# Batch 0: other queues and places for v's second half, the first w_in loads, the decay transposes and the first GEMM blocks

## The chip, the cores and the metric

The kernel runs on one core of a Trainium2 chip. The core has a matrix engine (TensorE, PE in the profile; its weight loads are PEld), VectorE (DVE), ScalarE (ACT), GpSimd (POOL) and SyncE (SP), each with its own instruction queue that is worked off in order, and 16 DMA engines that all queues of transfers share. SyncE and GpSimd both issue transfers here. The metric is the device time of one execution in microseconds: before the change the median of three runs is 336.82 us (336.6 to 336.88).

## The reference, cut to what matters

Attention with a forget gate on 8 batches, 8 heads, 576 tokens and 64 columns a head, and then an MLP with exact GELU on the 4608 tokens of 512 columns:

```python
scores = scale * np.matmul(q, k.transpose(0, 1, 3, 2))
log_f = np.log(np.clip(f, 0.0001, 1.0))
cum = np.cumsum(log_f, axis=-1)
decay = cum[:, :, :, None] - cum[:, :, None, :]
scores = np.where(causal, -1000000000.0, scores + decay)
attn = softmax(scores)
x = np.matmul(attn, v)                      # heads side by side: 4608 x 512
h = x @ w_in                                # 512 -> 2048
out = (0.5 * h * (1.0 + erf(h / sqrt(2)))) @ w_out   # 2048 -> 512
```

## The kernel before, in words

The order of all work is written out by hand; each engine runs its instructions in program order, and waits are put where data or buffers need them.

**Tiling.** A batch's 576 tokens are five blocks of up to 128 keys (`K0` = 0, 128, 256, 384, 448; the last one overlaps and only its upper 64 rows count). Heads go in four pairs `i` of 128 columns. Scores stand with keys on the partitions: TensorE writes `s`, ScalarE's exponential gives `e` in bf16. The decay is taken into v: `wT` holds a weight for each key and head, and `weigh_v` multiplies v by it into `vw`, whose 65th column is the weight itself, so that the product of `e` and `vw` (`o`) gives numerator and denominator at once. VectorE divides, giving `x`; TensorE transposes `x` into a PSUM tile `ps_x`, which is copied into `xT`. `gemm1` multiplies `xT` by a 128-column block `ffb` of w_in, four contraction steps `kt` of one pair each, and ScalarE's GELU makes `g`; the second GEMM multiplies `g` by w_out.

**Stages.** Batch 0 (`first_attention`) is attention alone, since nothing else is there yet to compute. Each later batch's attention is interleaved with the second GEMM of the batch before. The change is all in batch 0 and in the loads that precede it.

**Loads.** GpSimd issues q and k (converted to bf16 on the way) in four pieces each for batch 0, then all of w_in and w_out. `load_v` (line 114) makes one transfer for each block of keys, 128 KB for four heads. Lines 157 to 159 give SyncE nine of them: blocks 0 to 3 of heads 0 to 3, the same of heads 4 to 7, and block 4 of all heads. They come after GpSimd's memset of one column of `v_sb` (line 156).

**Batch 0 in order.** TensorE transposes q and k by pairs (`transposes(i, 0)` for q, `transposes(i, 1)` for k), computes scores in pieces (`scores_a`, `scores_b`, `scores_c`, `scores_t`, `scores_t4`), and transposes `decay` into `psw` by five small transposes (lines 711 to 715), from which VectorE copies `wT`. `keep()` is a filler: one matmul of 512 columns into a tile that nobody reads (ps_w, line 720). VectorE weighs v for heads 0 to 3 (lines 740, 741), GpSimd for heads 4 to 7 (lines 746, 747), and block 4 of all heads in one product (line 749). GpSimd's first two w_in loads stand behind the "gate" of lines 742 and 743, a copy of one column that must wait for block 3 of v's first four heads. Behind them in GpSimd's queue come the two weighings, w_in(2), the product of block 4, batch 1's first q and k, a memset of v's column for batch 1 and batch 1's v. `attend_0(i, h)` is the product of `e` and `vw` for one head; `to_xT_0(i, copy)` transposes and copies x of pair i.

**PSUM.** Three pools of two buffers each: `s_psum` (two banks a buffer) for scores, `o_psum` for attention products ("AV"; `spare()` takes one for a GEMM block), and `m_psum` for transposes and GEMM blocks.

**Into the first GEMM.** Lines 781 to 787: blocks 0, 1 and 2 are begun with their first three contraction steps, block 0 in `m_psum`, 1 and 2 in the halves of one `s_psum` tile `more`; then x of pair 3 is transposed and copied; then the three blocks get their fourth step, each followed by its GELU; block 3 is done whole. After block 4 comes `attend_tail` (the last 64 queries) and after block 5 `tail_0`.

Of the kernel before, what the change touches and what calls it, by code (L numbers as in the profile page):

```python
# [9 lines left out]
FP32 = mybir.dt.float32  # L10
# [5 lines left out]
P = 128  # L16
# [3 lines left out]
HP = 4  # L20
NBLK = 5
# [32 lines left out]
def kernel(  # L54
# [10 lines left out]
    nc = tc.nc  # L65
# [20 lines left out]
    x_pool = ctx.enter_context(tc.tile_pool(name="x", bufs=3))  # L86
# [27 lines left out]
    v_sb = consts.tile([P, H, NBLK, D], FP32)  # L114

    def load_v(b, h0=0, h1=H, eng=nc.sync, ns=range(NBLK)):
        if b >= B:
            return
        for n in ns:
            p0 = D if n == NBLK - 1 else 0  # L120
            eng.dma_start(
                v_sb[p0:P, h0:h1, n, :],
                v[b, h0:h1, K0[n] + p0 : K0[n] + P].rearrange("h p d -> p h d"),
            )
# [30 lines left out]
    diagonal(ident_fp, Alu.not_equal, 1.0, 0)  # L155
    nc.gpsimd.memset(v_sb[:, :, 0, 0:1], 0.0)
    load_v(0, 0, 4, ns=range(4))
    load_v(0, 4, 8, ns=range(4))
    load_v(0, ns=[NBLK - 1])

    qT = [consts.tile([P, S], BF16, name=f"qT{i}") for i in range(HP)]
    kT = [consts.tile([P, S], BF16, name=f"kT{i}") for i in range(HP)]
# [6 lines left out]
    def load_w_in(c):  # L169
        f4 = slice(c * d_ff // 4, (c + 1) * d_ff // 4)  # L170
        nc.gpsimd.dma_start(w_in_sb[:, :, f4], w_in_r[:, :, f4])
# [20 lines left out]
    def warm_up(n, w=TC):  # L192

        ps = m_psum.tile([P, TC], FP32, tag="m", name="ps_w")
        for _ in range(n):
            nc.tensor.matmul(
                ps[:, 0:w], warm[:, 0:P], warm[:, 0:w], start=True, stop=True
            )
# [4 lines left out]
    def transposes_first(b, i, which, pool, tag, parts=1):  # L203

        src = qk_of[b][which]
        ps = pool.tile([P, JT, PT], BF16, tag=tag, name="ps_f")
        for j in range(JT):
            for h in range(2):
                nc.tensor.transpose(  # L209
                    ps[h * D : (h + 1) * D, j, :],  # L210
                    src[:, 2 * i + h, j * D : (j + 1) * D],
                    ident_bf[:PT, :PT],
                )

        dst = (qT, kT)[which][i].rearrange("d (p j) -> d p j", j=JT)
        src = ps.rearrange("d j p -> d p j")
        if b or i:
            for p in range(parts):
                part = slice(p * PT // parts, (p + 1) * PT // parts)
                nc.vector.tensor_copy(dst[:, part], src[:, part])  # L220
        else:
            nc.vector.tensor_copy(dst[:, 0 : PT // 2], src[:, 0 : PT // 2])
            nc.scalar.copy(dst[:, PT // 2 :], src[:, PT // 2 :])
# [36 lines left out]
    def vw(b):  # L260
        if b not in vw_of:
            vw_of[b] = v_pool.tile([P, H, NBLK, D + 1], BF16, tag="vw", name=f"vw{b}")
        return vw_of[b]

    def weigh_v(b, i, eng=nc.gpsimd, n0=0, n1=NBLK):

        hs = slice(2 * i, 2 * i + 2)
        bh = b * H + 2 * i
        w = wT[:, n0:n1, bh : bh + 2].rearrange("p n h -> p h n")
        eng.tensor_tensor(  # L270
            vw(b)[:, hs, n0:n1, 0:D],
            v_sb[:, hs, n0:n1, :],
            w.unsqueeze(3).to_broadcast([P, 2, n1 - n0, D]),
            Alu.mult,
        )
        if b:
            eng.tensor_copy(vw(b)[:, hs, :, D], w)
# [75 lines left out]
    def xT(b):  # L353
        if b not in xT_of:
            xT_of[b] = xT_pool.tile([P, n_dm, XC], BF16, tag="xT", name="xT")
        return xT_of[b]
# [25 lines left out]
    def gemm1(c, ffb, kts=range(4), ps=None, act=True):  # L382
        src = xT(c) if c < B else tails
        if ps is None:
            ps = m_psum.tile([P, TC], FP32, tag="m", name="ps1")
        for kt in kts:
            nc.tensor.matmul(  # L387
                ps,
                w_in_sb[:, kt, ffb * P : (ffb + 1) * P],
                src[:, kt, 0:TC],  # L390
                start=(kt == 0),
                stop=(kt == n_dm - 1),
            )
        if n_dm - 1 in kts and act:
            gelu(c, ffb, ps)
        return ps

    def spare():
        return o_psum.tile([P, TC], FP32, tag="o", name="ps1")

    def gelu(c, ffb, ps):
        if c not in g_of:
            g_of[c] = [
                g_pool.tile([P, TC], BF16, tag=f"g{n}", name=f"g{n}")
                for n in range(n_ff)
            ]
        nc.scalar.activation(g_of[c][ffb], ps, Act.Gelu)  # L407
# [203 lines left out]
    def scores_a(i):  # L611
        scores_0([(i, 0, 0, TC)], new_e(0))

    def scores_b(i):
        scores_0([(i, 1, P, TC - P), (i, 3, 3 * P, P)], new_e(2))

    def scores_c(i):
        scores_0([(i, 2, 2 * P, 2 * P), (i + 1, 2, 2 * P, 2 * P)], new_e(3))

    def scores_t(i):  # L620
        parts = [(ii, n, TC, TL) for ii in (i, i + 1) for n in range(NBLK - 1)]
        scores_0(parts, new_e(3))

    def scores_t4():
        scores_0([(i, NBLK - 1, TC, TL) for i in range(HP)], e4[0][:, :, D:])
# [62 lines left out]
    def first_attention():  # L688

        most = NBLK - 1  # L690

        def transposes(i, which, parts=1):
            transposes_first(0, i, which, m_psum, "m", parts)

        warm_up(9)
        for which in range(2):
            transposes_first(0, 0, which, o_psum, "o")
        nc.vector.tensor_tensor_scan(
            decay[:, S - 2 :: -1],
            f_sb[:, S - 1 : 0 : -1],  # L700
            none[:, 0 : S - 1],
            2.0**80,
            Alu.mult,
            Alu.add,
        )
        warm_up(2, 2 * P)
        scores_a(0)
        scores_b(0)
        transposes(1, 0)
        transposes(1, 1, 2)  # L710
        psw = o_psum.tile([P, NBLK, BH], FP32, tag="o", name="psw")
        for n in range(NBLK):
            nc.tensor.transpose(
                psw[:, n, :], decay[:, K0[n] : K0[n] + P], ident_fp[:BH, :BH]
            )
        idle = o_psum.tile([P, TC], FP32, tag="o", name="ps_w")

        def keep(n=1):
            for _ in range(n):
                nc.tensor.matmul(idle, warm[:, 0:P], warm, start=True, stop=True)  # L720

        keep()
        scores_a(1)
        nc.vector.tensor_copy(wT[:, 0:4, :], psw[:, 0:4, :])
        nc.vector.tensor_copy(wT[D:P, 4, :], psw[D:P, 4, :])
        nc.vector.tensor_copy(
            vw(0)[:, :, :, D], wT[:, :, 0:H].rearrange("p n h -> p h n")
        )
        transposes(2, 0)
        scores_b(1)  # L730
        transposes(2, 1)
        keep()
        scores_c(0)
        transposes(3, 0)
        keep()
        scores_a(2)
        transposes(3, 1)
        keep()
        scores_b(2)
        weigh_v(0, 0, nc.vector, 0, most)  # L740
        weigh_v(0, 1, nc.vector, 0, most)
        g = x_pool.tile([P, 1], FP32, tag="gate", name="gate")
        nc.gpsimd.tensor_copy(g, v_sb[:, 3, most - 1, 0:1])
        load_w_in(0)
        load_w_in(1)
        weigh_v(0, 2, n1=most)
        weigh_v(0, 3, n1=most)
        load_w_in(2)
        nc.gpsimd.tensor_tensor(
            vw(0)[:, :, most, 0:D],  # L750
            v_sb[:, :, most, :],
            wT[:, most, 0:H].unsqueeze(2).to_broadcast([P, H, D]),
            Alu.mult,
        )
        load_qk_tokens(1, 0, 4)
        nc.gpsimd.memset(v_sb[:, :, 0, 0:1], 0.0)
        load_v(1, 0, 4, nc.gpsimd)
        load_w_in(3)
        load_qk_tokens(1, 4, 8)
        load_v(1, 4, 8, nc.gpsimd)  # L760
        keep()
        scores_a(3)
        keep()
        attend_0(0, 0)
        attend_0(0, 1)
        scores_b(3)
        scores_c(2)
        attend_0(1, 0)
        attend_0(1, 1)
        to_xT_0(0, nc.scalar.copy)  # L770
        scores_t(0)
        attend_0(2, 0)
        attend_0(2, 1)
        to_xT_0(1, nc.scalar.copy)
        scores_t(2)
        attend_0(3, 0)
        to_xT_0(2, nc.vector.tensor_copy)
        attend_0(3, 1)
        scores_t4()

        pss = [gemm1(0, 0, range(HP - 1))]
        more = s_psum.tile([P, 2, 512], FP32, tag="s", name="ps1")
        pss += [gemm1(0, ffb, range(HP - 1), more[:, ffb - 1]) for ffb in (1, 2)]
        to_xT_0(3, nc.vector.tensor_copy)
        for ffb in range(3):
            gemm1(0, ffb, (HP - 1,), pss[ffb])
        gemm1(0, 3)

    def gemm1_begin(b, both):

# [213 lines left out]
```

## Time and profile before

| What | Value |
|---|---|
| Median of three runs | 336.82 us |
| The profiled execution | 336.63 us, span 334.9 us |
| TensorE busy | 326.7 us, 98% of the span |
| VectorE, ScalarE, GpSimd busy | 184.1, 205.8, 128.7 us |
| Software queue (GpSimd's loads) | 17344 packets, 14.81 MB |
| SyncE's queue | 82512 packets, 28.34 MB |
| v loads of batch 0, issue to landing | 2.9 to 5.3 us |
| First two w_in loads issued at | 14.93 and 15.70 us |
| First matmul of the first GEMM | 21.48 us |

The profile is of one execution, its times counted from the start of the span. A line of the timeline gives start, length, engine, line of the kernel, operation, the tile written and the tiles read, the shape, how many instructions are merged, and in brackets how long the engine was idle before and what ended that. The chain of waits follows the work that ended last back through whatever released it. In the views of the DMA queues, q0 software_dynamic is GpSimd's queue and q1 hardware_dynamic SyncE's; a queue's line gives packets, MB and the share of the time of all 16 engines, which can exceed 100% where packets overlap.

### The profile page before, as it was taken

How to read it: one execution, taken by the hardware profiler on the slowest of the kernel's cores; microseconds unless marked ns; L12 is line 12 of the kernel's file. 1: busy time of each engine (PE TensorE's matmuls, PEld its weight loads, DVE VectorE, ACT ScalarE, POOL GpSimd, SP SyncE). 2: the span in 40 equal slices, each digit the busy share in tenths (PEclk: the TensorE clock that was granted, in tenths of full speed). 3: DMA queues.
4: the chain of work that ended last, by engine and by line, in shares of the span. 5: the costliest groups of instructions: out<-in, count | busy, mean ns of one | idle time of the engine just before them, and what ended most of it. 6: DMA issues, size and time to landing. Idle time of an engine off the chain costs nothing.

```text
span 334.9 us, 7881 instructions
## 1 busy us (share of the span) xinstructions
PE 326.7 (98%) x3195; PEld 170.3 (51%) x3195; DVE 184.1 (55%) x428; ACT 205.8 (61%) x295; POOL 128.7 (38%) x254
## 2 busy tenths in 40 slices
PE   7999999999999999999999999999999999999995
PEld 3664555445554466445644565456544654444443
DVE  5851666664449844894589548954796450020011
ACT  4785886984635786478827892798278846404600
POOL 7297873038327054714453355424441420000000
PEclk9999999999999999999999999999999999999999
DMA  7999999969999898499969795959700351021023
GB/s 115 188 184 217 209 193 140 189 119 177 216 196 167 126 207 168 103 141 187 187 118 142 147 195 148 133 111 213 176 1 2 94 61 52 0 78 50 0 46 82
DMA packets 100292, 44.18 MB, mean 132 GB/s; under 512 B 78784, under 2 KB 95424, under 8 KB 100256
## 3 DMA queue, kind: packets, MB, share of 16 engines
q1 hardware_dynamic: 82512, 28.34, 43.3%
q0 software_dynamic: 17344, 14.81, 29.4%
q8 instruction: 25, 0.41, 0.5%
q10 hardware_dynamic: 400, 0.52, 0.4%
q14 instruction: 11, 0.09, 0.1%
HBM read 36.85 MB, written 9.44 MB: 138 GB/s over the span
## 4 chain that ended last, share of the span: by engine, by line
PE 94%; DMA 2%; ACT 1%; POOL 1%; issue 1%; DVE 1%; DVEq 0%; POOLq 0%
PE ps L387 37%; PE ps L491 27%; PE ps L431 8%; PE o L332 8%; PE s L301 7%; DMA k<-in_k_dram 2%; PE ps_f L209 1%; PE s L601 1%; PE ps L551 1%; PE ps L527 1%; PE o L632 1%; ACT e L606 1%; PE ps_w L720 1%; ACT e L311 0%; POOL q L109 0%
## 5 line engine op out<-in xcount | busy, mean ns | idle before, releaser
L407 ACT ACTIVATE g<-ps 128x512 bf16<-128x512 f32 x138 | 78.7, 601 | 82.0 <-PE ps L387 81.5
L387 PE MATMUL ps<-xT,w_in_sb 128*128 128x512 bf16 x512 | 114.1, 379 | 1.5 <-ACT g L407 1.0
L491 PE MATMUL ps<-w_out_sb,g 64*128 64x512 bf16 (+1 forms) x711 | 108.1, 377 | 0.0
L311 ACT ACTIVATE e<-s 128x896 bf16<-128x896 f32 x112 | 87.7, 836 | 21.1 <-PE s L301 18.6
L387 PEld LDWEIGHTS <-w_in_sb 128*128 128x128 bf16 x576 | 55.4, 98 | 68.8 <-issue 4.7
L313 POOL TENSOR_SCALAR_AFFINE_SELECT e<-e 128x256 bf16<-128x256 bf16 (+1 forms) x135 | 49.1, 383 | 91.2 <-ACT e L311 91.0
L491 PEld LDWEIGHTS <-g 64*128 64x128 bf16 (+1 forms) x711 | 39.4, 95 | 34.7 <-issue 4.2
L270 POOL TENSOR_TENSOR vw<-v_sb,wT 128x640 bf16<-128x640 f32 (+1 forms) x30 | 38.2, 1275 | 25.3 <-DMA v_sb<-in_v_dram 15.1
L251 DVE COPY kT<-tk 64x288 bf16<-64x288 bf16 x96 | 43.8, 456 | 1.6
L251 DVE COPY qT<-tq 64x288 bf16<-64x288 bf16 x96 | 38.8, 405 | 3.7 <-DMA tq<-q 2.3
L499 DVE COPY ot<-ps 128x512 f32<-128x512 f32 x20 | 13.8, 691 | 47.3 <-PE ps L491 47.3
L301 PE MATMUL s<-qT,kT 64*128 64x256 bf16 (+1 forms) x336 | 37.0, 276 | 0.6 <-DVE kT L220 0.4
L332 PEld LDWEIGHTS <-e 128*128 128x128 bf16 x840 | 30.3, 98 | 7.9 <-POOL e L313 2.5
L440 DVE COPY ot<-ps 128x512 f32<-128x512 f32 (+2 forms) x9 | 5.7, 632 | 49.7 <-PE ps L431 49.7
L332 PE MATMUL o<-vw,e 128*128 128x65 bf16 x840 | 32.3, 194 | 0.0
L346 DVE TENSOR_TENSOR x<-o,r 128x320 bf16<-128x320 f32 x56 | 27.5, 491 | 2.7 <-DMA xT<-x 0.9
L431 PE MATMUL ps<-w_out_sb,g 128*128 128x512 bf16 (+2 forms) x144 | 28.0, 355 | 0.0
L301 PEld LDWEIGHTS <-kT 64*128 64x128 bf16 x336 | 16.6, 94 | 19.2 <-issue 4.2
L431 PEld LDWEIGHTS <-g 128*128 128x128 bf16 x144 | 13.5, 98 | 14.5
L511 DVE TENSOR_TENSOR ot<-ot,ps 128x512 f32<-128x512 f32 x22 | 15.1, 685 | 1.1
L345 DVE RECIPROCAL r<-o 128x5 f32<-128x5 f32 x56 | 10.5, 187 | 9.1 <-PE o L332 9.1
L387 PE MATMUL ps<-tails,w_in_sb 128*128 128x512 bf16 x64 | 14.3, 377 | 0.0
(91 smaller groups left out, 185.0 us busy)
## 6 DMA issues: line engine op xcount, KB each, us to landing
out_dram<-ot SPq DMA_DIRECT2D x32, 256.0 KB, 2.4
v_sb<-in_v_dram SPq DMA_DIRECT2D x24, 256.0 KB, 4.9
q<-in_q_dram POOLq DMA_DIRECT2D x6, 576.0 KB, 6.7
k<-in_k_dram POOLq DMA_DIRECT2D x6, 576.0 KB, 8.9
w_in_sb<-in_moe_w_in_dram POOLq DMA_DIRECT2D x4, 512.0 KB, 7.7
w_out_sb<-in_moe_w_out_dram POOLq DMA_DIRECT2D x4, 512.0 KB, 7.7
v_sb<-in_v_dram SPq DMA_DIRECT2D x15, 128.0 KB, 4.9
v_sb<-in_v_dram POOLq DMA_DIRECT2D x8, 128.0 KB, 7.6
```

Source lines behind the costliest of these rows:

```text
L251: nc.vector.tensor_copy(rows[:, odd], src[odd * D : (odd + 1) * D, 2 * i + h].rearrange("d j p -> d p j"),)
L270: eng.tensor_tensor(vw(b)[:, hs, n0:n1, 0:D], v_sb[:, hs, n0:n1, :], w.unsqueeze(3).to_broadcast([P, 2, n1 - n0, D]), Alu.mult,)
L301: nc.tensor.matmul(to, *ab, start=half < 0, stop=half == 1 or not masked)
L311: nc.scalar.activation(et[:, :, z:c], st[:, :, z:c], Act.Exp, scale=scale)
L313: nc.gpsimd.affine_select(out=et[:, :, c0 + z : c0 + P], in_=et[:, :, c0 + z : c0 + P], compare_op=Alu.is_ge, fill=0.0, base=z, pattern=[[ ...
L332: nc.tensor.matmul(o[:, m, :], e_of[b, i, t][:, h, c : c + P], vw_of[b][:, 2 * i + h, n, :], start=(n == 0), stop=(n == m),)
L346: nc.vector.tensor_tensor(x_of[b, i][:, :, h, :], o[:, :, 0:D], r.unsqueeze(2).to_broadcast([P, NBLK, D]), Alu.mult,)
L387: nc.tensor.matmul(ps, w_in_sb[:, kt, ffb * P : (ffb + 1) * P], src[:, kt, 0:TC], start=(kt == 0), stop=(kt == n_dm - 1),)
L407: nc.scalar.activation(g_of[c][ffb], ps, Act.Gelu)
L431: nc.tensor.matmul(pss[ts][:, c0:c1], g_of[c][kt][:, ts * P : (ts + 1) * P], w_out_sb[:, kt, c0:c1], start=(kt == 0), stop=(kt == n_ff - 1),)
L491: nc.tensor.matmul(banks[r], g_of[c][kt][rows, ts * P : (ts + 1) * P], w_out_sb[rows, kt, :], start=kt == (steps.index("r") if r else 0), ...
L511: nc.vector.tensor_tensor(ot, ot, bank, Alu.add)
```

## The change

Four things, all in batch 0:

- v's second half (blocks 0 to 3 of heads 4 to 7) is issued by GpSimd instead of SyncE, and v's block 4 by GpSimd too, between w_in(0) and w_in(1); the gate is gone, so w_in(0) is issued right behind v's second half.
- The decay transposes come before the k transposes of pair 1 instead of after, and the first of the fillers, the one ahead of `scores_a(1)`, is gone.
- x of pair 3 is transposed after two begun blocks of the first GEMM instead of three.
- Block 3 is begun like the others, in a buffer of `o_psum`, and all four are then finished in order.

```diff
     nc.gpsimd.memset(v_sb[:, :, 0, 0:1], 0.0)
     load_v(0, 0, 4, ns=range(4))
-    load_v(0, 4, 8, ns=range(4))
-    load_v(0, ns=[NBLK - 1])
+    load_v(0, 4, 8, nc.gpsimd, range(4))
...
         transposes(1, 0)
-        transposes(1, 1, 2)
         psw = o_psum.tile([P, NBLK, BH], FP32, tag="o", name="psw")
         for n in range(NBLK):
             nc.tensor.transpose(
                 psw[:, n, :], decay[:, K0[n] : K0[n] + P], ident_fp[:BH, :BH]
             )
+        transposes(1, 1, 2)
...
-        keep()
         scores_a(1)
...
         weigh_v(0, 0, nc.vector, 0, most)
         weigh_v(0, 1, nc.vector, 0, most)
-        g = x_pool.tile([P, 1], FP32, tag="gate", name="gate")
-        nc.gpsimd.tensor_copy(g, v_sb[:, 3, most - 1, 0:1])
         load_w_in(0)
+        load_v(0, 0, 8, nc.gpsimd, [most])
         load_w_in(1)
...
         pss = [gemm1(0, 0, range(HP - 1))]
         more = s_psum.tile([P, 2, 512], FP32, tag="s", name="ps1")
-        pss += [gemm1(0, ffb, range(HP - 1), more[:, ffb - 1]) for ffb in (1, 2)]
+        pss += [gemm1(0, 1, range(HP - 1), more[:, 0])]
         to_xT_0(3, nc.vector.tensor_copy)
-        for ffb in range(3):
+        pss += [gemm1(0, 2, range(HP - 1), more[:, 1])]
+        pss += [gemm1(0, 3, range(HP - 1), spare())]
+        for ffb in range(4):
             gemm1(0, ffb, (HP - 1,), pss[ffb])
-        gemm1(0, 3)
```

## The prediction

> **What bounds the kernel now.** I read the page's head first, then the chain of waits over the first 30 us, then what waited for what around two places of it, and last the DMA queues by stretches.
>
> ```profile
> span 334.9 us, 7881 instructions
> PE 326.7 (98%) x3195; PEld 170.3 (51%) x3195; DVE 184.1 (55%) x428; ACT 205.8 (61%) x295; POOL 128.7 (38%) x254
> ```
>
> TensorE is busy for 98% of the span: what a change is worth is the stall that it takes from or gives to TensorE. In the waits of TensorE after 30 us there are only 0.4 and 0.2 us; the change sits before that, in batch 0. The chain there (start, length, what):
>
> ```profile
> 14.86 0.41 PE s L601 x6
> 15.26 0.32 PE ps_w L720
> 15.59 0.71 PE o L632 x20
> ...
> 21.55 2.05 PE ps L387 x9
> 23.60 0.24 PE ps_x L656 x4
> 23.83 0.02 issue
> 23.86 0.44 DVE xT L659
> 24.29 0.04 issue
> 24.34 0.39 PE ps L387
> 24.73 0.02 issue
> 24.75 1.09 ACT g L407 x2
> ```
>
> TensorE is fed from 8.5 to 23.8 us, but partly with fillers (ps_w L720), and at 15.5 the first attention product (o L632) starts just as its operand is ready. The timeline of that place (start, length, engine, ..., idle before and what ended it):
>
> ```profile
> 14.69 0.19 POOL L743 COPY gate<-v_sb 128x1 f32<-128x1 f32 x1 [6.75 <-DMA v_sb<-in_v_dram]
> 14.76 1.29 DVE L270 TENSOR_TENSOR vw<-v_sb,wT 128x512 bf16<-128x512 f32 x2 [0.25 <-DMA v_sb<-in_v_dram]
> 15.51 0.79 PE L632 MATMUL o<-vw,e 128*128 128x65 bf16 x20
> 24.34 0.59 PE L387 MATMUL ps<-xT,w_in_sb 128*128 128x512 bf16 x2 [0.52 <-DVE xT L659]
> 25.89 0.38 PE L387 MATMUL ps<-xT,w_in_sb 128*128 128x512 bf16 x1 [0.96 <-ACT g L407]
> ```
>
> So v's first half (heads 0 to 3, blocks 0 to 3) lands by 14.69. VectorE, which has waited 0.25 us for it, weighs two pairs of heads in 1.29 us, so the first pair is ready near 15.45 and TensorE begins at 15.51. That landing has no slack worth naming: whatever delays it delays the attention of batch 0 and all behind it. The two stalls at 24.34 and 25.89 are the other thing that the change touches.
>
> How the two DMA queues share the engines is told by three stretches: SyncE's queue (hardware_dynamic) alone at 11 to 12 us, both at 60.5 to 62.5 us (transposing loads of SyncE against a w_out load of GpSimd), and SyncE's alone just after, at 63 to 65 us. Columns: packets, MB, share of 16 engines.
>
> ```profile
> q1 hardware_dynamic: 1111, 0.28, 126.4%
> ...
> q0 software_dynamic: 284, 0.29, 87.6%
> q1 hardware_dynamic: 290, 0.07, 33.8%
> ...
> q1 hardware_dynamic: 1683, 0.42, 125.2%
> ```
>
> Together the queues get the same number of packets, 284 and 290, though GpSimd's are four times as large; SyncE's falls from 842 packets a us to 145. A big packet on GpSimd's queue buys as much of a turn as a small one on SyncE's.
>
> **The change part by part.** The profiled execution took 336.63 us, 0.19 less than the median of 336.82; sums are made against 336.63 and 0.19 is added at the end.
>
> *Last x behind two blocks, fourth block in an AV bank.* Now nine partial products (2.05 us, 0.228 each), then four transposes (0.24), and TensorE waits 0.52 us for VectorE's copy (0.42). After: six products (1.37), the transposes, then six more (1.37), which cover copy and wait. Gain 0.52. The next wait, 0.96 us, stays: block 2 is finished in the half of the tile `more` beside the half that block 1's GELU reads, and TensorE resumes at 25.89, as the second GELU ends (24.75 + 1.08), not the first; that order is unchanged. Were it to go too, 1.48 would be gained; were nothing covered, 0. I take 0.52. The AV bank costs nothing: its last reader on VectorE is through at 21.14, and tail_0, the next to want it, comes some 1.5 us after the GELU that frees it.
>
> *Decay transposes sooner, one filler less.* The five decay transposes (0.45) start behind the q transposes at 8.2, in a 0.32 us wait for k, so the k transposes start 0.06 to 0.1 late; the filler (0.32) goes. Scores of pair 1 start 0.1 to 0.2 sooner, but the next thing late is v at 15.5, so this is worth 0 unless v comes sooner. Bounds: 0.3 gain, 0.1 loss. Taken: 0.
>
> *The loads.* SyncE issues nine v loads from 7.97 to 14.85; after, four, out by 10.1. GpSimd sat idle 6.75 us up to the gate; there it now issues v's second half (four loads at 0.76), w_in(0), block 4 and w_in(1), from about 8.2 to 13.5, before it waits for anything; w_in(0) goes out 3.6 us and w_in(1) 3.0 us sooner. The 5.3 us of issuing lie in the idle time. Behind them on GpSimd's queue stand its two weighings (2.08), w_in(2), the product of block 4 and batch 1's loads; TensorE needs the first weighing only at 18.43. w_in(0) landed by 21.36 for a use at 21.48: it comes sooner, worth 0 by itself.
>
> What the gate's absence costs: in the trace w_in's packets never meet v's first half. Now they do. v's first half is 4 x 512 packets of 256 bytes (0.28 MB are 1111 of them); meeting it are 128 packets of 4 KB (a v load through GpSimd moves 0.25 MB in 94 packets at 28.9 to 29.9 us), 512 of 1 KB for w_in(0), 32, 512 for w_in(1), and 512 for w_in(2) once the weighings are through near 17. One for one, SyncE's queue goes at 145 packets a us: 2048 / 145 = 14.1 us from 10.0, when its first packets moved, so v lands near 24.5 and not 14.6: 9.8 us late. Lower end: 0 (SyncE's four loads, issued first, are served first). Within the one-for-one case at least 5 us: 1184 packets are queued before GpSimd first waits (1024 at 145 a us, 160 at 94 a us: 8.8 us, to about 19); the other 864 of SyncE's then need 0.8 us at 1111 a us. Upper end 10.8 (one engine was held 1.25 us by a 16 KB instruction packet near 11.9 us). I take 9.8, since the stretch at 60.5 is the only one with both queues full for long.
>
> [...]
>
> With TensorE idle for 10 us comes a second cost. The nine first matmuls after the start took 4.02 us, 0.43 each, against 0.228 at 21.5; if the long idle time brings that pace back, 2.0 us are lost again, if not, 0. The longest stall in the trace, 0.96 us, shows no slow pace; 10 us is nearer to a start, but half of what follows is paced by ScalarE's exponentials (1.95 and more): I take 1.0. [...]
>
> Sum: 336.63 - 0.52 + 9.8 + 1.0 + 0.19 = 347.1, say 347.0.
>
> **The rivals.** *v is on time (faster or same).* SyncE's loads are issued at 7.97, 8.44, 8.99, 9.54, GpSimd's from 8.2 at 0.76 apart, the third only at 9.7; if the four are served before GpSimd's are queued in earnest, v lands by 15 and the change keeps its 0.52 plus up to 0.2 from the front: 336.2, range 335.8 to 336.6. For it: at 10 to 12 us SyncE moved 1726 packets beside GpSimd's 125. Against it: GpSimd's queue was then running dry (482 packets in the 2 us before, SyncE's none, though its loads were out), and now it does not. It decides where v's first half lands before about 15.0.
>
> *Sharing by time or bytes.* v's two halves, each 0.5 MB, go side by side. At 0.28 MB a us both are through about 3.7 us after 10.0; the first half, alone 1.9 us long, is late by up to 1.9, or 0.7 if half of it has gone first, 2.8 if w_in(0) takes some of its turns. Net of 0.52: 336.9 to 339.1, likeliest 337.8. For it: the total of bytes is unchanged, and SyncE's issue stalls (1.35 and 1.53 us in its fifth and seventh load) go. Against: the 284 to 290.
>
> *The gate's absence does nothing, as GpSimd gets to its loads late.* Against: it was idle 6.75 us there; folded into the first rival.
>
> **How the numbers follow.** One packet for one, TensorE waiting for v: 0.49, at 347.0, its own range 341.3 (v 5.0 us late, no slow pace) to 349.1 (10.8 late, 2.0 lost). v on time: 0.29. Sharing by bytes: 0.22. A measurement here tells 0.2%, 0.67 us: below 336.15 is faster, above 337.49 slower. Of the first rival 0.16 is faster and 0.13 same; of the second 0.06 same and 0.16 slower. So faster 0.16, same 0.19, slower 0.65. The range runs from 336.0, below which lies half of the faster part (0.08), to 349.0 (0.06 above).
>
> **What the changed profile would show.** Right: VectorE's first weighing (L270) idles for a DMA until 20 to 25 us; TensorE shows one wait of 5 to 10 us before o L632; GpSimd's memset before batch 1's v loads, which overwrites what VectorE reads, waits likewise; w_in(0) lands well before v; while both queues are full their packets are equal in number. At gemm1's start there is no wait for xT, and the wait of about 1.0 for the GELU remains. Wrong: the first weighing starts before 16; then the first rival holds at 15.0 or less, the second between. The prediction falls if SyncE's loads keep more than 145 packets a us beside GpSimd's, or if they are through before GpSimd's queue fills.

## The result and the profile after

| | before | after |
|---|---|---|
| median of 16 executions each, on one chip | 336.84 us (336.06 to 337.40) | 337.51 us (337.00 to 338.86) |
| ratio | | 1.0032, 95% interval 1.0019 to 1.0044 |
| the profiled execution | 336.63 us, span 334.9 | 338.85 us, span 337.0 |
| v's first half has landed | 14.64 us | 16.22 us |
| first attention product begins | 15.51 | 17.09 |
| first matmul of the first GEMM | 21.48 | 24.23 |
| five blocks of that GEMM done, the tail's attention products begin | 27.92 | 29.99 |

Slower by 0.3%: the forecast sign, but 0.67 us and not the 10.2 that were forecast (347.0). The time lies in the range of the second rival, sharing by time or bytes (336.9 to 339.1, likeliest 337.8); whether its reason held is another question, answered below.

The chain of waits of the changed kernel over the stretch (start, length, what):

```profile
9.60 6.63 DMA v_sb<-in_v_dram
...
16.35 0.70 DVE vw L269
17.05 0.04 issue
17.09 0.79 PE o L631 x20
17.88 1.50 PE s L600 x24
...
24.30 1.40 PE ps L386 x6
25.70 0.22 PE ps_x L655 x4
25.92 1.52 PE ps L386 x7
27.45 0.02 issue
27.47 1.09 ACT g L406 x2
28.56 0.04 issue
28.60 1.46 PE ps L386 x6
30.06 0.76 PE o L666 x38
```

Two things are new against the chain of before. It goes through a DMA: SyncE's fourth v load, 6.63 us from its issue to its landing, where TensorE's own work had stood. And where the chain had VectorE's copy of x (xT) between the partial products, it now goes straight on, six products, four transposes, seven products, up to the wait for the GELU (ACT g), which stayed. The timeline shows the first of the two close up (last bracket: idle before, and what ended it):

```profile
16.35 2.16 DVE L269 TENSOR_TENSOR vw<-v_sb,wT 128x512 bf16<-128x512 f32 x2 [2.07 <-DMA v_sb<-in_v_dram]
16.62 2.80 POOL L269 TENSOR_TENSOR vw<-v_sb,wT 128x512 bf16<-128x512 f32 x2 [3.09 <-DMA v_sb<-in_v_dram]
17.09 0.79 PE L631 MATMUL o<-vw,e 128*128 128x65 bf16 x20 [1.75 <-DVE vw L269]
```

VectorE's idle time before the first weighing is 2.07 us and not 0.25, and TensorE waits 1.75 us for it. Both halves of v come at once, so VectorE and GpSimd weigh at the same time: VectorE's two weighings take 2.16 us instead of 1.29 (0.69 and 1.55), GpSimd's 2.80 instead of 2.08.

By stages the profiled execution adds up: +1.58 to the attention's begin, +1.17 from there to the first GEMM (7.14 us for 5.97), -0.68 in that GEMM (5.76 for 6.44), nothing behind it that matters (6.71 from there to the first scores of batch 1 in both). That is 2.07 of the 2.1 us between the spans. The +1.17 is mostly a thing of its own, to be seen in the stretches cut at the steps of the granted clock (PE, PEld, DVE, ACT and POOL busy, then PEclk, DMA share, GB/s):

```profile
14.55:17.97 3.42, 1.67 (x30) 1.09 (x31) 1.62 (x2) 1.72 (x2) 1.35 (x2) 1.00 1.18 216
17.97:21.38 3.41, 3.41 (x64) 2.93 (x60) 2.69 (x9) 2.27 (x3) 3.39 (x4) 0.50 0.99 153
21.38:24.79 3.41, 3.41 (x91) 2.72 (x86) 2.55 (x9) 3.11 (x5) 3.12 (x6) 1.00 1.13 176
```

After the stretch with 1.67 us of TensorE work in 3.42, TensorE ran 3.41 us at half clock (0.50). Five of the 16 executions, the profiled one among them, have a mean granted clock of 0.993 to 0.995 (338.45 to 338.86 us); in the other eleven it is 0.998 or more, and their median is 337.40.

### The profile page after: what moved, and what is told of

Same layout as the page of the kernel before. It is cut to its first block, busy times and chain, and to the rows that moved or that the text cites. A ratio compares the mean times of both kernels' runs of the same rounds, so it can differ in the third digit from the quotient of the medians.

```text
span 337.0 us, 7874 instructions
## 1 busy us (share of the span) xinstructions
PE 327.4 (97%) x3194; PEld 171.2 (51%) x3194; DVE 184.6 (55%) x428; ACT 205.9 (61%) x295; POOL 133.2 (40%) x258
## 4 chain that ended last, share of the span: by engine, by line
PE 90%; DMA 5%; POOL 2%; ACT 1%; issue 1%; DVE 1%; SPq 0%; POOLq 0%; DVEq 0%
PE ps L386 37%; PE ps L490 25%; PE ps L430 8%; PE o L331 8%; PE s L300 7%; DMA xT<-x 3%; DMA v_sb<-in_v_dram 2%; PE o L631 1%; PE ps L550 1%; PE s L600 1%; PE ps L526 1%; POOL q L109 1%; PE ps_f L208 1%; POOL k L109 1%; ACT e L310 0%
## 5 line engine op out<-in xcount | busy, mean ns | idle before, releaser
L269 POOL TENSOR_TENSOR vw<-v_sb,wT 128x640 bf16<-128x640 f32 (+1 forms) x30 | 38.9, 1298 | 25.0 <-PE ps L386 11.9
L250 DVE COPY kT<-tk 64x288 bf16<-64x288 bf16 x96 | 42.8, 445 | 1.6
L605 ACT ACTIVATE e<-s 128x1024 bf16<-128x1024 f32 (+1 forms) x13 | 12.5, 990 | 4.1 <-PE s L600 3.7
```

The costliest lines, as they stand in the source:

```text
L250: nc.vector.tensor_copy(rows[:, odd], src[odd * D : (odd + 1) * D, 2 * i + h].rearrange("d j p -> d p j"),)
L269: eng.tensor_tensor(vw(b)[:, hs, n0:n1, 0:D], v_sb[:, hs, n0:n1, :], w.unsqueeze(3).to_broadcast([P, 2, n1 - n0, D]), Alu.mult,)
```

## The experiments

Medians stand against those of before in the same group of runs: 336.91 for the first eight, 336.74 for e9 and e10. What is called v's first half is blocks 0 to 3 of heads 0 to 3.

### The parts alone

*e1: the loads and the gate of before, the new places of decay transposes and filler, and the new GEMM order.*

```diff
 (the changed kernel, with)
-    load_v(0, 4, 8, nc.gpsimd, range(4))
+    load_v(0, 4, 8, ns=range(4))
+    load_v(0, ns=[NBLK - 1])
...
+        g = x_pool.tile([P, 1], FP32, tag="gate", name="gate")
+        nc.gpsimd.tensor_copy(g, v_sb[:, 3, most - 1, 0:1])
         load_w_in(0)
-        load_v(0, 0, 8, nc.gpsimd, [most])
```

> All loads and the gate as before; only the decay transposes, the missing filler and the new order of the first GEMM blocks. My theory: the loss of the change is all in the loads, and the compute part gains the 0.5 us stall before the fourth contraction step: 336.2 to 336.4 against 336.8 before, no wait of PE for xT, v's first half landing at 14.6 as before. Rival (the new order of the GEMM blocks costs as much as it gains, or the missing filler hurts): 336.8 or more.

Measured: 336.49, ratio 0.9993 (0.9971 to 1.0014). In its profile (336.39) v's first half lands at 14.23, the GEMM stage is 5.76 long, and the wait for xT is gone.

*e2: the loads of the change alone, the rest as before.*

```diff
 (the kernel before, with)
-    load_v(0, 4, 8, ns=range(4))
-    load_v(0, ns=[NBLK - 1])
+    load_v(0, 4, 8, nc.gpsimd, range(4))
...
-        g = x_pool.tile([P, 1], FP32, tag="gate", name="gate")
-        nc.gpsimd.tensor_copy(g, v_sb[:, 3, most - 1, 0:1])
         load_w_in(0)
+        load_v(0, 0, 8, nc.gpsimd, [most])
```

> Only the loads of the change: v's second half and block 4 on GpSimd's queue, no gate; compute as before. My theory: v's first half lands 1 to 1.6 us late (near 16), TensorE waits 1 to 1.8 us before the first attention product, and the time is 337.8 to 338.1 where the clock holds and about 1.5 us more where it falls to half. Rival (the loss comes from the compute part): 336.6 to 336.9.

Measured: 338.21, ratio 1.0032 (1.0012 to 1.0053), 1.3 us by the medians. v's first half lands at 15.86. TensorE's three longest waits from 8 to 32 us (who waited and for what: us in total, times, longest):

```profile
PE o L631 <- DVE vw L269: 1.3, 1, 1.3
PE ps L386 <- ACT g L406: 1.0, 1, 1.0
PE ps L386 <- DVE xT L658: 0.5, 1, 0.5
```

One new wait of 1.3 us for v, and the old waits of the GEMM. The loads carry the whole loss.

*e7: the new GEMM order alone.*

```diff
 (the kernel before, with)
-        pss += [gemm1(0, ffb, range(HP - 1), more[:, ffb - 1]) for ffb in (1, 2)]
+        pss += [gemm1(0, 1, range(HP - 1), more[:, 0])]
         to_xT_0(3, nc.vector.tensor_copy)
-        for ffb in range(3):
+        pss += [gemm1(0, 2, range(HP - 1), more[:, 1])]
+        pss += [gemm1(0, 3, range(HP - 1), spare())]
+        for ffb in range(4):
             gemm1(0, ffb, (HP - 1,), pss[ffb])
-        gemm1(0, 3)
```

> The kernel before with the new order of batch 0's first GEMM alone (last x behind two blocks, fourth block in an AV bank). As forecast: 0.52 us sooner, 336.3. As the changed kernel's profile has it (the stage from the first partial product to the end of that GEMM is 5.76 long and not 6.44): 0.68 sooner, 336.15. Rival, the gain is given back behind: 336.8. No wait for xT in any case, the wait for the GELU near 1.0; v's first half at 14.6 as before.

Measured: 336.44, ratio 0.9981 (0.9959 to 1.0002), 0.47 us by the medians, with an interval that just takes in no change. TensorE's two longest waits in its profile (336.31):

```profile
PE ps L387 <- ACT g L407: 1.0, 1, 1.0
PE s L601 <- issue: 0.8, 2, 0.6
```

The wait for xT is gone, that for the GELU is there, the stage is 5.76 long: 0.68 gained at that place. Ahead of it there is a new stall of 0.6 us before the last scores ("issue": no wait that the profile shows), taken up in e10. Loads and GEMM order together give +1.3 - 0.47 = 0.83, beside 0.67 measured for the whole change.

### Why v is late

*e3: the change, with the gate back ahead of w_in(0).*

```diff
 (the changed kernel, with)
+        g = x_pool.tile([P, 1], FP32, tag="gate", name="gate")
+        nc.gpsimd.tensor_copy(g, v_sb[:, 3, most - 1, 0:1])
         load_w_in(0)
         load_v(0, 0, 8, nc.gpsimd, [most])
```

> The change with the gate put back ahead of w_in(0): w_in waits until block 3 of v's first four heads has landed, v's second half stays on GpSimd's queue. Theory one (v's own second half takes the turns, w_in is behind it and harmless): v's first half lands as in the change, 15.5 to 16.2, time as the change, 337.3 to 337.7, or more if w_in(0) now lands after 21.5. Theory two (w_in without its gate is what delays v): v's first half back to 14.6 to 15.0, TensorE's wait gone, 336.3 to 336.6.

Measured: 337.67, ratio 1.0028 (1.0008 to 1.0048), as without the gate: by the times, w_in behind v's second half is not the cause. The one profiled execution is an odd one (341.47 us; a filler of 512 columns takes 0.61 us at 16.23 and 18.09, and 0.39 only from 20.62), but its v loads went out within 0.7 us of the changed kernel's, and its gate opened early:

```profile
14.99 0.19 POOL L741 COPY gate<-v_sb 128x1 f32<-128x1 f32 x1 [2.96 <-DMA v_sb<-in_v_dram]
```

v's first half had landed by 14.93, 4.6 us after its fourth load went out (10.29), beside 6.6 in the changed kernel, 5.9 in e2 and 6.4 in e5, and 4.0 to 5.1 where SyncE loads all of v and the gate holds w_in back (before, e1, e7, e10). Each v load of batch 0 shows 16 landings in the traces before and after the change, as many as there are DMA engines, and VectorE starts 0.12 us (before) and 0.13 us (changed kernel) after the last one of the fourth load: at 14.76 after 14.64, and at 16.35 after 16.22. The eighth of the 16 came 3.5 us after the issue of the fourth load before the change and 3.1 to 3.3 in e1, e7 and e10, 5.1 in the changed kernel, 4.6 and 4.8 in e2 and e5, and 4.3 here. So with v's second half on the other queue most landings of the first half come later, behind a gate too. The last landings are another matter: here no w_in was under way yet and the 16 KB packet of the instruction queue came at 14.31, behind v, while in the changed kernel w_in was under way and that packet came at 12.54, amid v, and took 1.30 us. How much of the 1.58 us each of these makes was not separated, and the times of the other twelve executions don't show so early a v.

*e4: the halves exchanged, the first on GpSimd's queue and the second on SyncE's.*

```diff
 (the changed kernel, with)
-    load_v(0, 0, 4, ns=range(4))
-    load_v(0, 4, 8, nc.gpsimd, range(4))
+    load_v(0, 4, 8, ns=range(4))
+    load_v(0, 0, 4, nc.gpsimd, range(4))
```

> The change with the halves of v exchanged: the first half (needed first) on GpSimd's queue, the second on SyncE's. If the queues share by bytes, about 128 KB in turn, the first half lands as in the change, 15.5 to 16.2, and the time is 337.3 to 337.7. If a packet counts as a turn, GpSimd's 4 KB packets win and the first half lands by 14.0, with 336.2 to 336.5, and SyncE's half comes after 18 and holds GpSimd's weighing up.

Measured: 339.02, ratio 1.0060 (1.0041 to 1.0079). The timeline:

```profile
15.66 2.52 POOL L269 TENSOR_TENSOR vw<-v_sb,wT 128x512 bf16<-128x512 f32 x2 [1.95 <-DMA v_sb<-in_v_dram]
16.33 2.40 DVE L269 TENSOR_TENSOR vw<-v_sb,wT 128x512 bf16<-128x512 f32 x2 [1.88 <-DMA v_sb<-in_v_dram]
17.32 0.79 PE L631 MATMUL o<-vw,e 128*128 128x65 bf16 x20 [1.80 <-DVE vw L269]
```

Neither queue wins by much: SyncE's half is through at 15.50, GpSimd's at 16.21, in the changed kernel 16.22 and 16.46. Packet for packet GpSimd's half, a sixteenth of the packets by the prediction's count, would have been through long before. The time expected for sharing by bytes, 337.3 to 337.7, was missed: four of the nine executions have a granted clock of 0.993 or 0.994, and the median of the other five is still 338.49. What else costs there is open.

*e6: the kernel before without the gate: all of v on SyncE's queue, w_in alone beside it.*

```diff
 (the kernel before, with)
-        g = x_pool.tile([P, 1], FP32, tag="gate", name="gate")
-        nc.gpsimd.tensor_copy(g, v_sb[:, 3, most - 1, 0:1])
```

> The kernel before without the gate: all of v stays on SyncE's queue, w_in(0) and w_in(1) go out on GpSimd's queue from about 8.3 us, as 1 KB packets beside v's 256-byte ones. Sharing by bytes (or load by load): v's first half is late by as much as behind v's second half in the changed kernel, landing at 15 to 16.5; attention begins 16 to 17.3, and the time is 337.3 to 339.5. One packet for one: 1024 packets of w_in at 145 a us hold SyncE's queue until near 17, v's first half lands at 17.5 to 19 and the time is 339.5 to 342. If the gate does nothing at all: v by 14.9, 336.8.

Measured: 344.26, ratio 1.0209 (1.0185 to 1.0233). v's first half lands at 21.0, later than either case had it, and TensorE waits:

```profile
PE o L632 <- DVE vw L270: 6.6, 1, 6.6
```

This is the picture that the prediction painted of the change, and it took another load to bring it about. Sharing by bytes falls here: SyncE got 0.08 MB beside 0.29. The queues of four kernels, in stretches in which both were full (packets, MB, share of 16 engines). The changed kernel from 12 to 14 us, v's second half on GpSimd's queue (q0), the first on SyncE's (q1):

```profile
q1 hardware_dynamic: 786, 0.19, 59.5%
q0 software_dynamic: 95, 0.26, 56.2%
```

e6 from 14 to 16 us, w_in in packets of 1 KB on q0:

```profile
q0 software_dynamic: 290, 0.29, 85.4%
q1 hardware_dynamic: 337, 0.08, 30.2%
```

*e9: as e6, but w_in(0) and w_in(1) in pieces of 128 columns, so that a run of contiguous bytes is 256 and not 1024 bytes long.*

```diff
 (e6, with)
-        nc.gpsimd.dma_start(w_in_sb[:, :, f4], w_in_r[:, :, f4])
+        step = P if c < 2 else d_ff // 4
+        for j in range(f4.start, f4.stop, step):
+            fj = slice(j, j + step)
+            nc.gpsimd.dma_start(w_in_sb[:, :, fj], w_in_r[:, :, fj])
```

> The kernel before without the gate, as in the run in which w_in alone went beside v on GpSimd's queue (344.26 us, v's first half at 21.0), but w_in(0) and w_in(1) are each loaded in four pieces of 128 columns: the same bytes at the same place, in runs of 256 bytes and not of 1 KB. Theory, the queues take turns run for run of contiguous bytes, and v through GpSimd is 16 such runs in each 4 KB packet: SyncE's v now gets about half of the bytes again (100 to 140 KB a us at 12 to 14 us, and not 22 to 36), v's first half lands at 15 to 16.5, and the time is 337.3 to 340. Rival, what counts is how much is queued on GpSimd, or that it is w_in: v's first half again lands at 19 to 21 and the time is 342 to 345. Issuing is eight loads of about 0.8 us on GpSimd and not two, done by 15, in its idle time.

Measured: 344.95, ratio 1.0241 (1.0215 to 1.0267). The queues from 12 to 14 us:

```profile
q0 software_dynamic: 593, 0.15, 75.0%
q1 hardware_dynamic: 820, 0.20, 59.3%
```

SyncE has more than half of the bytes again, 0.20 MB for 0.08, and v's first half lands at 17.41 and not at 21.0. So it is not w_in as such, nor how much of it is queued, that held v in e6, but the length of its runs. (The eight pieces also went out over 6 us and not 1.5, which this run doesn't part from it; e11 puts the length to the test from the other side.) The expectation of 15 to 16.5 and of the time missed: the two queues together moved 184 GB/s, where the changed kernel moved 236, and the second half of v, still behind on SyncE's queue, landed only at 24.22, so that a second wait took what the first gave back:

```profile
PE o L635 <- DVE vw L273: 3.0, 1, 3.0
PE o L635 <- POOL vw L273: 2.8, 1, 2.8
```

*e11: as e6, but w_in by blocks of rows: runs of 4 KB, in packets as large as those of v in the changed kernel.*

```diff
 (e6, with)
-        f4 = slice(c * d_ff // 4, (c + 1) * d_ff // 4)
-        nc.gpsimd.dma_start(w_in_sb[:, :, f4], w_in_r[:, :, f4])
+        nc.gpsimd.dma_start(w_in_sb[:, c, :], w_in_r[:, c, :])
```

> The kernel before without the gate, as in the run in which w_in alone went beside v (v's first half at 21.0; SyncE 22 to 46 KB a us at 12 to 17 us, packets 150 to 91 up to 153 to 162), but w_in is loaded by its four blocks of rows and not of columns: the same bytes a load, in runs of 4 KB, a quarter as many packets. If a turn is one contiguous run (and v's 4 KB packets on GpSimd's queue counted for 8 turns because each gathers 16 runs of 256 bytes), SyncE again gets one packet for one: 10 to 30 KB a us while w_in flows, v's first half at 17 to 19.5. If a turn goes by bytes once packets are as large as 4 KB, or load by load, SyncE gets a third to a half of the bytes (70 to 140 KB a us) and v's first half lands at 15 to 16.5. All four parts of w_in are needed by the first partial products' ends, so the whole is longer than with columns, 345 or more; the time tells nothing here.

Measured: 354.27 in a single run. v's first half landed at 20.90, later than the 17 to 19.5 expected for one packet for one. The queues from 14 to 16 us:

```profile
q0 software_dynamic: 97, 0.37, 94.9%
q1 hardware_dynamic: 98, 0.02, 9.2%
```

97 packets to 98, and SyncE is left with 12 KB a us. A packet of 4 KB goes with one of SyncE's here, and in the changed kernel a packet of up to the same 4 KB goes with 8 (786 to 95; 12 if one counts only the 63 packets of 4 KB that 0.26 MB can fill). What differs is what is in them: w_in's are one contiguous run of 4 KB into one partition, v's through GpSimd hold, by the kernel's layout, 16 runs of 256 bytes, each for a partition of its own. Counted in runs, 0.26 MB are 1016 of 256 bytes, beside 786 of SyncE's; in e2, whose stretch has 0.25 MB in 86 packets against 889, 977 to 889. Run for run holds within a factor of 1.4 in all four (290 to 337, 593 to 820, 97 to 98, 1016 to 786); bytes for bytes and packet for packet each fail in some. It is a count that fits these stretches; by what the engines choose between the queues no run shows.

*e12: v divided by blocks, GpSimd with two loads of 256 KB for SyncE's four of 128.*

```diff
 (e8 below, with)
-    for h0 in (0, 4):
-        load_v(0, h0, h0 + 4, ns=(0, 1))
-        load_v(0, h0, h0 + 4, nc.gpsimd, (2, 3))
+    load_v(0, 0, 8, nc.gpsimd, (2, 3))
+    for h0 in (0, 4):
+        load_v(0, h0, h0 + 4, ns=(0, 1))
```

> The changed kernel with v divided by blocks: SyncE loads blocks 0 and 1 in four loads of 128 KB, heads 0 to 3 first, GpSimd blocks 2 and 3 in two loads of 256 KB, all heads in each. In the run with v divided the same way in loads of 128 KB on both queues, the queues moved 156, 70 and 115 KB (GpSimd) against 145, 139 and 124 KB (SyncE) a us from 11 to 14 us. If the queues take turns load for load, GpSimd's larger loads get two bytes for SyncE's one: 150 to 180 against 75 to 95 KB a us from 11 to 14. If by runs or bytes, the shares stay about equal and SyncE's four loads are through by 15.5. In both cases TensorE's first attention product waits for GpSimd's second load, whole, at 15.5 to 16.5, and the time is 337.2 to 338.8, no sooner than the changed kernel.

Measured: 341.88 in a single run beside 339.01 for before. From 11 to 14 us GpSimd moved 176, 119 and 128 KB a us and SyncE 94, 112 and 80: the first figure is that of load for load, the second that of equal shares, and the mean, 141 to 95, lies between. So this run doesn't tell the two apart. The time was lost elsewhere, and the expectation missed it:

```profile
PE o L632 <- POOL vw L270: 3.0, 1, 3.0
PE o L632 <- DVE vw L270: 1.3, 1, 1.3
```

SyncE's last v load landed at 21.60: of its packets 84, 47, 37, 17 and 9 a us went from 15 to 20 us, beside 179 to 200 a us of GpSimd's. So what was left of a load with short runs went slowly once longer ones had come up on the other queue; why was not shown.

### The half clock

*e5: the changed kernel with eight fillers instead of one ahead of the first attention product.*

```diff
 (the changed kernel, with)
-        keep()
+        keep(8)
         attend_0(0, 0)
```

> The changed kernel with eight fillers instead of one ahead of the first attention product, so that TensorE has some 1.8 us of work (7 more at about 0.25) in the 1.75 us that it waits for v's first half. Theory, the idle window trips the clock: the stretch of 3.4 us at half clock from 18 us goes, every execution has a mean granted clock of 0.998 or more, and the group of times at 338.4 to 338.9 is gone; the median is 337.0 to 337.4. v's first half still lands near 16.2 and the attention begins near 17.1 to 17.5. Rival, the clock falls for another reason: the stretch and the upper group stay, median 337.4 to 338.2. If the fillers delay the attention, 0.2 to 0.5 us are added in either case.

Measured: 337.31, ratio 1.0016 (1.0002 to 1.0029). v's first half lands at 16.18 as before, but the fillers fill the wait:

```profile
15.13 1.90 PE L719 MATMUL ps_w<-warm 128*128 128x512 bf16 x8
...
17.05 0.79 PE L631 MATMUL o<-vw,e 128*128 128x65 bf16 x20
```

In all twelve executions the mean granted clock is 0.997 or more and the highest time is 338.15, against 338.86. Were the share still 5 in 16, twelve in a row without the half clock would come about once in 90 times, so the idle time very likely brought it on. It is not the only way: two of 61 executions of the kernel before in these groups (340.01 us at 0.995, 340.0 at 0.990) and one of e1 (339.68 at 0.994) have a low clock too, and were not profiled. From the attention's begin to the GEMM it is 6.31 us now: 0.83 of the 1.17 was the clock, by these two profiles. The other 0.34 goes with the simultaneous weighings (TensorE waits 0.4 us for VectorE's x there, which comes behind them). Three of the twelve, at 338.1 with a full clock, stay unexplained.

### What would have been better

*e8: both queues load first what is needed first.*

```diff
 (the changed kernel, with)
-    load_v(0, 0, 4, ns=range(4))
-    load_v(0, 4, 8, nc.gpsimd, range(4))
+    for h0 in (0, 4):
+        load_v(0, h0, h0 + 4, ns=(0, 1))
+        load_v(0, h0, h0 + 4, nc.gpsimd, (2, 3))
```

> The changed kernel with v divided otherwise: SyncE loads blocks 0 and 1 and GpSimd blocks 2 and 3, both of heads 0 to 3 first and of heads 4 to 7 after; no gate, w_in(0) right behind on GpSimd's queue as in the changed kernel. Theory, v's first half is late because the second half takes every other turn ahead of it: now only what is needed first is queued first, v's first half lands at 13.5 to 14.9, attention begins by 15.6, there is no half-clock stretch, and the time is 335.9 to 336.5, sooner than both kernels. Rival, w_in or the number of queues makes v late: it lands at 15.5 to 16.5 again and the time is 337.2 to 338.2.

Measured: 336.79, ratio 1.0001 (0.9989 to 1.0013).

```profile
14.63 1.29 DVE L270 TENSOR_TENSOR vw<-v_sb,wT 128x512 bf16<-128x512 f32 x2 [0.32 <-DMA v_sb<-in_v_dram]
...
17.65 2.08 POOL L270 TENSOR_TENSOR vw<-v_sb,wT 128x512 bf16<-128x512 f32 x2 [4.41 <-DMA v_sb<-in_v_dram]
...
18.76 0.79 PE L632 MATMUL o<-vw,e 128*128 128x65 bf16 x20 [0.41 <-POOL vw L270]
...
22.30 0.20 PE L601 MATMUL s<-qT,kT 64*128 64x64 bf16 x1 [0.76 <-issue]
```

The first weighing starts at 14.63 with no gate and two queues, as the theory has it: the late v of the change (16.22) came from the order, the second half moving beside what was needed first. (With half of its loads on each queue v's first half is also through earlier, 14.45, so less of it meets w_in and the instruction packet, here at 13.74.) The time expected, 335.9 to 336.5, was missed. Nothing was left of the GEMM's gain, for two new waits: 0.41 us for GpSimd's weighing (v's second half, its SyncE part beside w_in, landed at 17.48, though 15 of the 16 landings had come by 15.72), and 0.76 before the last scores.

*e10: the new GEMM order alone, w_in(1) issued behind GpSimd's weighings.*

```diff
 (e7, with)
         load_w_in(0)
-        load_w_in(1)
         weigh_v(0, 2, n1=most)
         weigh_v(0, 3, n1=most)
+        load_w_in(1)
         load_w_in(2)
```

> The kernel before with the new order of batch 0's first GEMM, and w_in(1) issued behind GpSimd's two weighings, near 18.4 us and not 15.1. In the profile of the new GEMM order alone TensorE stood 0.6 to 0.7 us before its last scores of batch 0, from 21.08 to 21.85, and an instruction packet of 16 KB began 19.48 and took 0.95. Theory, that packet is held up behind what is queued of w_in and TensorE waits for it: with w_in(1) later it begins before 19, the stand goes, and the time is 335.7 to 336.1. Rival, the stand is of another cause: it stays, and the time is 336.3 to 336.6. If w_in(1) comes too late for its use near 23, it is 0.3 to 1 us longer.

Measured: 336.32, ratio 0.9983 (0.9971 to 0.9994), the only one whose interval against before lies below 1. But not for the reason given:

```profile
21.93 0.20 PE L601 MATMUL s<-qT,kT 64*128 64x64 bf16 x2 [0.99 <-issue]
```

The stall is 0.99 us here. The 16 KB instruction packet went at 19.72, no sooner than in e7 (19.48), so what is queued of w_in(1) does not hold it up.

## Why the prediction was wrong

**The sign and the place: right.** TensorE's new wait is the one before o L632 (L631 now), VectorE's first weighing waits for v, the wait for xT went and that for the GELU stayed at 1.0, and the share of the loads (+1.3 by e2) is larger than the gain of the GEMM.

**The step that failed** is the sentence "A big packet on GpSimd's queue buys as much of a turn as a small one on SyncE's", as it was used for "128 packets of 4 KB". As a count of packets it fits one-run packets: the stretch at 60.5 us (1 KB rows of w_out, 284 to 290), e6 (290 to 337), e11 (97 to 98) and, less closely, e9 (593 to 820). It does not fit v's packets on GpSimd's queue (95 to 786). Counted as runs, v's second half was 2048 and not 128, and the queues shared about evenly: 0.19 MB to 0.26. SyncE went at some 390 packets a us, not at 145, and the 9.8 us came out at 1.58 in the profile and 1.22 in e2's. "At least 5 us" fell with it, since it counted the same packets one for one. The 9.8 was too large even by the prediction's own counts: the 1696 packets that it has on GpSimd's queue run out before SyncE's 2048, which gives a landing near 22.6, 8.0 late (and 14.1 from 10.0 is 24.1, not 24.5).

The bound that the prediction drew for its second rival, 0.7, 1.9 and 2.8 us of lateness, held. Its reason, equal shares by time or bytes, does not hold in general (e6 by bytes, 0.08 MB to 0.29; by time e6, 30.2% to 85.4%, and e11, 9.2% to 94.9%), only where the runs are of one length (the changed kernel, 0.19 MB to 0.26 and 59.5% to 56.2%; e9, 0.20 to 0.15 and 59.3% to 75.0%).

The prediction took one packet for as much as another. Here a packet of v on GpSimd's queue goes with 8.3 (786 to 95) to 10.3 (889 to 86, e2) of SyncE's packets of 256 bytes, and a packet of w_in with 1.2 at 1 KB (337 to 290, e6) and 1.0 at 4 KB (98 to 97, e11).

**The gate: wrong.** "What the gate's absence costs" was costed mostly on w_in's packets, three times 512. In the change v's second half stands between, and when w_in came up in numbers, after 14 us, only some 130 of SyncE's 2048 packets were left: gate or no gate, 337.67 and 337.51. (The last of them began at 15.69, and two of the fourth load's 16 landings came after 15.36, at 15.95 and 16.22; e3 leaves open how much of that is w_in.) Taken away alone (e6) the gate was worth 7.4 us: the number was near the one forecast, for another kernel, which is luck.

**The slow pace: there, but after a shorter stall.** It was put at 1.0 for 10 us of idle time, on the ground that the longest stall in the trace, 0.96, shows none. Behind a stall of 1.75 us it came in the profiled execution, at a cost of 0.83 by the profiles, and by the mean clock in 5 of 16, with 1.4 us between the medians of the two groups of times (338.85 and 337.40).

**The GEMM order: mis-sized.** 0.52 forecast, 0.68 measured in the stage (5.76 for 6.44, in the changed kernel as in e1, e7 and e10). The order hid the copy of x and cost nothing in turn. The 0.16 beyond can be read from the two chains: before, one product stands alone between the copy and the GELU and takes 0.39 (24.34), where products in a row take 0.23 each; in the changed chain none stands alone. The prediction counted the wait and not this. "The AV bank costs nothing" holds.

**The decay transposes and the filler: as taken,** as far as the intervals tell. e1, which has them, and e7, which has not, are 336.49 and 336.44.

**A term left out:** the weighings of VectorE and GpSimd fell together and took longer (VectorE's two 2.16 us for 1.29, its second 1.55 for 0.69; GpSimd's two 2.80 for 2.08); some 0.34 us of the stage go with it.

## What to carry to other kernels

Before you put a load on another queue to have it sooner, ask what is queued ahead of or beside the bytes that are needed first: splitting by queue what is needed at different times delayed the early part here (v's first half at 16.22 in the change, at 14.45 in e8). To estimate who wins, count contiguous runs and not packets or bytes, which was right here within a factor of 1.4: a queue of 256-byte runs was left with 12 KB a us beside 4 KB runs (e11). A gate that holds a load of long runs back until short ones have landed can be worth much (7.4 us in e6), and one ahead of loads that follow other short runs little or nothing (e3, 337.67 for 337.51). And price a stall of TensorE with the clock: behind one of 1.75 us TensorE ran 3.41 us at half clock in the profiled execution, which cost another 0.83.

## What the runs showed of the hardware

**The granted clock behind a stall.** In the changed kernel's profile the granted clock steps at 4.31, 17.97 and 21.38 us, 13.65 and 3.41 us apart. Cut from 4.31 us on into stretches of 3.41 us, the first three have TensorE busy for a share of 0.83 or more and the fourth, with the stall of 1.75 us, for 0.49; the fifth is at half clock, and the nine behind it, up to 52 us and each with 0.84 or more, are at full clock. In the profile of the kernel before the clock stays at 1.00 from 5.29 us on to the end of the work; in the same count from there, up to 53 us, the emptiest stretch (from 22.36 us) has TensorE busy for 0.60. In two other profiles twenty attention products that take 0.80 us before the change (at 17.11) are slow behind a stall too: 1.28 us at 19.34 in e4, whose stall is 1.80 us and whose mean clock is 0.994, and 1.26 and 1.21 us at 21.87 and 24.67 in e6, whose stall is 6.59 us and whose clock is 0.990. That 1.75 us brought the half clock only in some executions would follow if a stall had to lie in one such stretch; that is the author's estimate, and neither this nor how full a stretch has to be was shown: only one of those executions was profiled.

**Instruction packets.** The 25 packets of 16 KB on the instruction queue (q8) took 0.89 to 1.48 us each in the profile before and 0.88 to 1.98 in the changed kernel's. In the kernel before 15 of the 16 landings of v's first half had come by 13.81 and the last came at 14.64; such a packet had begun at 11.89 and took 1.25, and that it delayed this landing is inferred. And in e1, e7, e8 and e10 TensorE stood 0.6 to 1.0 us before the last scores of batch 0, in e7 and e10 to 1.4 and 1.2 us after the end of the next such packet (20.43, then 21.85; 20.7, then 21.93). Before the change the packet was through at 20.0 and TensorE passed the place at 21.3 without a stall. This looks like TensorE waiting for its instructions; it was not shown, and what delays the packet is open. It would explain why e8's early v brought so little.
